# Values of the later chunks fetched by casting transfers of GpSimd in an attention and feed-forward kernel

## The chip, the cores and the metric

The kernel runs on one core of one Trainium2 chip. Time is device time of one execution, in microseconds (us). The engines have the names of the profile: PE (TensorE, matmuls) with PEld (its weight loads), DVE (VectorE), ACT (ScalarE), POOL (GpSimd) and SP (SyncE, which here only issues transfers). A transfer that SP or ACT issues is shown by the profile in a queue of kind hardware_dynamic (q1 for SP), one that POOL issues in q0, software_dynamic; both queues run on the same 16 DMA engines.

## The reference

Attention with two kinds of heads, then a gated feed-forward layer. Four batches, 8 heads, 768 positions, 64 values per head; heads 0, 2 and 6 see all earlier positions, the others ("streaming") see only the first 4 positions (the sink) and the last 64 (the window).

```python
scores = scale * np.matmul(q, k.transpose(0, 1, 3, 2))
stream_keep = causal & (is_sink | in_win)
mask = np.where(retr[0, :, 0, 0, None, None], full_mask, stream_mask)
scores = np.where(mask[None, :, :, :], scores, -1000000000.0)
a = np.exp(scores - max)
a = a / (np.sum(a, axis=-1, keepdims=True) + 1e-09)
attn_out = np.matmul(a, v)
x = attn_out.transpose(0, 2, 1, 3).reshape(B * S, H * D)   # 3072 x 512
h = x @ w_in                                               # 512 x 2048
g = h * (1.0 / (1.0 + np.exp(-beta * h)))
out = g @ w_out                                            # 2048 x 512
```

Inputs and output are float32; the products run in bfloat16.

## The kernel before

The 3072 rows are cut into 8 chunks of 384 positions: half a sequence of one batch each, in the order (batch 0, first half), (1, first), (0, second), (1, second), then the same for batches 2 and 3. Chunks are numbered from 0, so the fourth is chunk 3. Each chunk has 4 units, a unit being a pair of heads: unit u belongs to chunk u // 4. For each unit there is a step QK (scores, `steps_QK`, matmuls of line 451), an exponential on ACT into `es` (lines 458 and 460), masks by products on DVE (lines 478 to 496), a step PV (`steps_PV`, matmuls of line 532 into `po`), and a division by the sums (lines 541 and 545) into `x`. `x` is transposed into `xT` by a transfer of SP (line 560). Then the feed-forward layer of the chunk: `steps_G1` (line 600, gate in lines 605 and 608) and `steps_G2` (line 653), and an output by SP (line 659).

The order on the engines is written out. Up to unit 7 the string `RAMP` names each step by a word; from unit 8 on a loop runs over t = 8 to 33 and the string `PLAN` has a row for each t: the QK of unit t and the PV of unit t - 1 ("V", "p") are mixed with feed-forward steps of earlier chunks ("a", "b"). Work of the other engines is put off with `later(delay, fn)`: it is emitted once an estimated clock of the matmul stream has gone on by `delay` ns, or when the first step that needs it forces it. Each engine, and SP's and POOL's queue of transfers, then runs its own list in order; the semaphores between them are set by the framework. Eight transfers of one kind can be under way before the next waits for the oldest's semaphore.

What the change touches:

- Values. `VX[b % 2]` holds the values of a batch in bfloat16: six tiles of 128 positions, 8 heads, 64 values and a 65th column of ones, so the 64 values of one head stand 130 bytes from those of the next. `load_v` (line 132) has SP fetch a tile of 128 positions in float32 into the stage `vs` (256 KB); `cast_v` (line 251) casts it into `VX`, on an engine that the plan names, for chunk 3 on DVE and for chunks 4 to 7 on POOL (`values_at`).
- Sink blocks. `VO[b % 2]` holds for the streaming heads copies of value tiles in which the first 4 positions are replaced by the sequence's first 4. `sink_values` makes them on POOL: lines 259 (one copy of 128 partitions for each tile) and 260 (the 4 rows). A chunk of a first half has one block, of a second half three.
- Keys and queries of chunks 3 to 7. `load_rows` (line 282) has POOL fetch them by casting transfers, twelve a chunk, 64 KB as written, into buffers `ROWS[c % 2]` (named `s` in the profile, after the stage whose memory they use). `transposes_dma` (lines 294 and 297) has SP transpose them into `KT` and `QTD`. A row load into a buffer waits until the transposes that read it have run.
- Readers. PV of a unit reads `VX` and `VO` (line 532); the first unit of a chunk (heads 0 and 2) reads only `VX`, the second is the first to read `VO`.

In the loop before the change, chunk c's value tile i is loaded by SP at t = 4c - 4 + i (delay 2500) and cast at t = 4c - 3 + i (delay 3000); with the third cast come the sink copies. Chunk 3's loads stand in `RAMP` (words `lv3.0g lv3.1 lv3.2`).

Of the kernel before, what the change touches and what calls it, by code (L numbers as in the profile page):

```python
# [18 lines left out]
def kernel(  # L19
# [13 lines left out]
    nc = tc.nc  # L33
    B, H, S, D = q.shape
# [4 lines left out]
    HALF = S // 2  # L39
    HT = HALF // 128  # L40
    NPAIR = H // 2
    NU = B * 2 * NPAIR
    NCHUNK = B * 2

    retr = [1, 0, 1, 0, 0, 0, 1, 0]
    n_sink_i = 4
# [26 lines left out]
    def later(delay, fn):  # L73

        todo = [fn]

        def once():
            if todo:
                todo.pop()()
        heapq.heappush(heap, (clock[0] + delay, count[0], once))  # L80
        count[0] += 1
        return once
# [5 lines left out]
    def step(s):  # L88
        cost, fn = s
        flush(clock[0])  # L90
        clock[0] += cost
        fn()


    chunks = [(b0 + i, h2) for b0 in range(0, B, 2) for h2 in range(2) for i in range(2)]
# [27 lines left out]
    def load_v(c, held=False, tiles=range(HT)):  # L123
        b, h2 = chunks[c]
        if tiles[0] == 0:
            staged["v", c] = stage.tile([128, HT, H, D], F32, name="vs")
        vs = staged["v", c]
        if held:
            nc.gpsimd.memset(vs[:, :, 0, 0:1], 0.0)
        for t in tiles:  # L130
            r = h2 * HALF + t * 128
            nc.sync.dma_start(out=vs[:, t], in_=v[b, :, r:r + 128, :].rearrange("h p d -> p h d"))  # L132
# [68 lines left out]
    VX = [kvp.tile([128, 2 * HT, H, D + 1], BF16, name=f"VX{b}") for b in range(2)]  # L201
# [38 lines left out]
    def cast(u, name, copy):  # L240
        b, h2, p = units[u]
        c = u // NPAIR
        s = st_u.setdefault(u, {})
        if "qkb" not in s:
            s["qkb"] = att.tile([128, 2, HT, 2, D], BF16, name="qkb", bufs=4)
        copy(out=s["qkb"][:, "qk".index(name)], in_=staged[name, c, p // 2][:, p % 2:4:2].rearrange("p h t d -> p t h d"))

    def cast_v(c, t, copy):

        b, h2 = chunks[c]  # L250
        copy(out=VX[b % 2][:, h2 * HT + t, :, 0:D], in_=staged["v", c][:, t])  # L251

    def sink_values(c):
        b, h2 = chunks[c]
        ka, kz = (1, 2) if h2 == 0 else (2, 5)
        vx, vo = VX[b % 2], VO[b % 2]
        copy = nc.gpsimd.tensor_copy if c < 2 else nc.gpsimd.tensor_copy
        for i in range(ka, kz):
            copy(out=vo[:, i - 1, :, 0:D], in_=vx[:, i, :, 0:D])  # L259
        copy(out=vo[0:n_sink_i, ka - 1:kz - 1, :, 0:D],  # L260
             in_=vx[0:n_sink_i, 0:1, :, 0:D].to_broadcast([n_sink_i, kz - ka, H, D]))

    chunk_values = {2: []}

    def values_at(c, t, delay):
        def go():
            cast_v(c, t, nc.vector.tensor_copy if c < 4 else nc.gpsimd.tensor_copy)
            if t == HT - 1:
                sink_values(c)
        chunk_values.setdefault(c, []).append(later(delay, go))  # L270

    def sinks_at(u, delay):
        st_u[u]["sinks"] = later(delay, lambda: sinks_of(u))
# [43 lines left out]
    def transpose_qk(u, name):  # L317

        s = st_u.setdefault(u, {})
        tp = ps_m.tile([128, 512], F32, name="mm").bitcast(BF16)[:, 0:HALF].rearrange("p (t j) -> p t j", t=HT)  # L320
        for t in range(HT):
            nc.tensor.transpose(tp[:, t, :], s["qkb"][:, "qk".index(name), t].rearrange("p h d -> p (h d)"), ident)  # L322
        s["t" + name] = tp
# [351 lines left out]
    h = FO // 2  # L675
# [10 lines left out]
    def run(steps):  # L686
        for x in steps:
            step(x)

    copies = {"v": nc.vector.tensor_copy, "a": nc.scalar.copy, "g": nc.gpsimd.tensor_copy}  # L690
# [5 lines left out]

    def do(word):

        what, n, i, eng = re.fullmatch(r"([a-z]{2}|[a-z][A-Z])(\d*)\.?(\d*)([vag]?)", word).groups()
        n, i = int(n or 0), int(i or 0)  # L700
        if what in ("ck", "cq"):
            cast(n, what[1], copies[eng])
        elif what in ("tk", "tq"):
            step((170, lambda: transpose_qk(n, what[1])))
        elif what in ("kk", "kq"):
            copy_qk(n, what[1], copies[eng])
        elif what == "ko":
            sinks_of(n)
        elif what in ("ad", "qk", "ex", "ma"):
            if n not in visits:  # L710
                visits[n] = steps_QK(n)
            step((0 if what in ("ex", "ma") else 170, lambda: visits[n][what](i)))
        elif what == "cv":
            cast_v(n, i, copies[eng])
        elif what == "vo":
            sink_values(n)
        elif what == "pv":
            pv = products.setdefault(n, [])
            if not pv:
                pv.extend(steps_PV(n))  # L720
            run(pv[:2])
            del pv[:2]
        elif what == "no":
            normalize(n)
        elif what == "xd":
            x_by_dma(n)
        elif what == "xx":
            run(steps_X(n))
        elif what == "cx":
            copy_x(n, copies[eng])  # L730
        elif what == "on":
            ones_v(engines[eng], n)
        elif what == "ne":
            negatives([(0, 1, 2), (3, 4)][n])
        elif what == "be":
            step((100, beta_go))
        elif what == "lv":
            load_v(n, held=eng == "g", tiles=[i])
        elif what == "lq":
            load_qk(n, i, held=eng == "g")  # L740
        elif what == "wi":
            load_w_in(n)
        elif what == "wo":
            load_w_out(n)
        elif what == "rq":
            rows_queries()
        elif what == "rk":
            rows_keys()
        elif what == "ro":
            if n not in more_rows:  # L750
                more_rows[n] = load_rows(n)
            more_rows[n].pop(0)()
        elif what in ("dk", "dq"):
            transposes_dma(n, what[1])
        elif what == "ml":
            late[n].pop(0)()
        elif what == "tt":
            run(steps_T(n))
        elif what == "zz":
            keep_busy(n)  # L760
        elif what == "hm":
            opened.append(done[0])
            done[0] += 1
            step(halves[0](opened[-1], 0))
        elif what == "hf":
            step(halves[0](opened.pop(0), 1))
        else:
            feed({"mm": "a", "mA": "A", "mb": "b"}[what])

    def feed(x):  # L770
# [19 lines left out]
        qk3.1 no1 pv2 ck6v ex3.0 cq5v ck5g pv2 tk6 xx0 ad4.0 cq6g pv3 kq4v ex3.1 pv2 ad4.1 cx0v ad5.0 qk4.1 pv3 lv2.2  # L790
        no2 on1g tq5 pv3 qk4.0 kk6a ml0 tk5 cq7g kq5v ex4.1 kk5a ko5 ko6 ad5.1 tq6 wi1 qk5.0 ex4.0 tk7 tq7 ex5.0 no3
        qk5.1 ex5.1 kq6v xx1 ad6.0 kk7v wi2 kq7v wi3 cx1a qk6.0 ml1 ad6.1 ex6.0 cv1.1g ko7 qk6.1 cv1.0v ex6.1 hm lq2.1
        ma5.0 ma5.1 mm cv1.2g vo1 mm wo0 pv4 lv3.0g ad7.0 lv3.1 pv4 hf pv4 no4 qk7.0 ad7.1 pv5 pv5 ex7.0 lv3.2 qk7.1
        pv5 no5 ml1 wo1 ex7.1 pv6 pv6 wo2 mm pv7 rq pv7 pv7 no7 wo3 pv6 no6 rk cq8g xx2 ro3 cx2a mA mA ck8g xx3 cx3a
        mm mA mm mA mm mm mA mm mm mm mA mm ro3 mm mm mA mm mm mm ro3 mA mm ro3 mA mm ro3 mm mm ro3 mA mA mb mb tt8 mb
        mb mb
# [36 lines left out]
    for t in range(8, NU + 2):  # L833
        c, i = (t + 5) // NPAIR, (t + 5) % NPAIR
        if t >= 14 and c < NCHUNK and i < 3:
            for x, f in enumerate(load_rows(c)[4 * i:4 * i + 4]):
                later(1000 + 1500 * x, f)
        c, i = (t + 4) // NPAIR, (t + 4) % NPAIR
        if t >= 12 and c < NCHUNK and i < HT:
            later(2500, lambda c=c, i=i: load_v(c, tiles=[i]))  # L840
        c, i = (t + 3) // NPAIR, (t + 3) % NPAIR
        if t >= 9 and c < NCHUNK and i < HT:
            values_at(c, i, 3000)
        if t > 14 and t % NPAIR == 2 and t // NPAIR + 1 < NCHUNK:
            transposes_dma(t // NPAIR + 1)
        if 12 <= t + 1 < NU:
            sinks_at(t + 1, 1000)
        qk = steps_QK(t) if t < NU else []
        pv = steps_PV(t - 1) if 8 <= t - 1 < NU else []
        xx = steps_X(5) if t == 13 else steps_X(NU // 2 - 1) if t == NU + 1 else []  # L850
        tr = steps_T(t + 1) if t + 1 < 12 else []

        plan = PLAN[t - 8]
        for x in plan.split():
            if x == "V":
                run(qk[:1])
                qk = qk[1:]
            elif x == "p":
                run(pv[:1])
                pv = pv[1:]  # L860
            elif x == "T":
                run(tr)
                tr = []
            elif x == "X":
                run(xx)
                xx = []
            elif len(x) > 1:
                do(x)
            else:
                feed(x)  # L870
        run(qk + tr + xx + pv)
    i = 0
# [39 lines left out]
```

## Time and profile before

| what | us |
|---|---|
| median of 3 runs (lowest, highest) | 228.2 (228.14, 228.51) |
| the profiled execution | 228.94 |
| its span, first to last instruction | 227.0 |
| PE busy in the span | 219.4 |
| ACT busy | 154.0 |
| DVE busy | 142.1 |
| POOL busy | 87.3 |

The granted clock of PE was 0.999 over the span. In the groups of the profile a row has the line, engine and operation, what is written and read, how often, the busy time and mean ns of one, and after the second bar the idle time of the engine just before these instructions with what ended it. In the DMA view a queue's row has its packets, megabytes and the time of its packets as a share of the 16 engines' time; packets overlap, so shares can add up to over 100%. In a timeline a row has the start, the length, and in brackets the idle time before. In the view of waits the numbers are the total, how often, and the longest.

### The profile page before, as it was taken

How to read it: one execution, taken by the hardware profiler on the slowest of the kernel's cores; microseconds unless marked ns; L12 is line 12 of the kernel's file. 1: busy time of each engine (PE TensorE's matmuls, PEld its weight loads, DVE VectorE, ACT ScalarE, POOL GpSimd, SP SyncE). 2: the span in 40 equal slices, each digit the busy share in tenths (PEclk: the TensorE clock that was granted, in tenths of full speed). 3: DMA queues.
4: the chain of work that ended last, by engine and by line, in shares of the span. 5: the costliest groups of instructions: out<-in, count | busy, mean ns of one | idle time of the engine just before them, and what ended most of it. 6: DMA issues, size and time to landing. Idle time of an engine off the chain costs nothing.

```text
span 227.0 us, 5019 instructions
## 1 busy us (share of the span) xinstructions
PE 219.4 (97%) x1898; PEld 126.4 (56%) x1917; DVE 142.1 (63%) x342; ACT 154.0 (68%) x254; POOL 87.3 (38%) x143
## 2 busy tenths in 40 slices
PE   7989999999999999999999999999999999999994
PEld 3555766654655665556654664556645655456553
DVE  4679888852684779357932699646963779028600
ACT  2698898946767897449933887569876878139621
POOL 5377952249163399143064049910670000000000
PEclk9999999999999999999999999999999999999999
DMA  6999999999999899989869779596963030111012
GB/s 204 262 301 239 225 197 198 195 220 171 149 216 178 161 153 144 141 175 133 103 131 162 126 151 140 92 133 103 216 64 107 24 81 0 49 46 46 0 49 92
DMA packets 95383, 31.66 MB, mean 139 GB/s; under 512 B 81776, under 2 KB 92416, under 8 KB 95360
## 3 DMA queue, kind: packets, MB, share of 16 engines
q1 hardware_dynamic: 58880, 22.82, 50.2%
q0 software_dynamic: 35904, 8.13, 41.9%
q10 hardware_dynamic: 576, 0.40, 0.6%
q8 instruction: 15, 0.25, 0.5%
q14 instruction: 8, 0.07, 0.1%
HBM read 27.27 MB, written 6.29 MB: 148 GB/s over the span
## 4 chain that ended last, share of the span: by engine, by line
PE 89%; DMA 4%; DVE 2%; SPq 2%; issue 1%; ACT 0%; ACTq 0%; DVEq 0%
PE mm L653 34%; PE mm L600 25%; PE sp L600 12%; PE sp L451 6%; PE po L532 6%; DMA s<-in_k_dram 3%; DMA s<-in_q_dram 2%; PE mm L638 2%; DVE es L478 1%; PE mm L322 1%; SPq L132 1%; PE mm L570 1%; PE mm L451 1%; SPq L119 1%; PE sp L422 1%
## 5 line engine op out<-in xcount | busy, mean ns | idle before, releaser
L653 PE MATMUL mm<-w_out_sb,gT 128*128 128x512 bf16 x349 | 84.1, 379 | 1.3 <-issue 0.5
L460 ACT ACTIVATE es<-sp 128x768 bf16<-128x768 f32 (+2 forms) x72 | 56.5, 837 | 19.6 <-PE sp L451 19.4
L600 PE MATMUL mm<-xT,w_in_sb 128*128 128x384 bf16 x348 | 64.6, 326 | 0.0
L600 PEld LDWEIGHTS <-w_in_sb 128*128 128x128 bf16 x512 | 47.8, 98 | 29.7 <-issue 0.2
L605 ACT ACTIVATE th<-mm,beta_h 128x384 f32<-128x384 f32 x87 | 49.8, 588 | 5.6 <-PE mm L600 0.9
L653 PEld LDWEIGHTS <-gT 128*128 128x128 bf16 x368 | 33.4, 98 | 36.0 <-issue 1.5
L608 DVE SCALAR_TENSOR_TENSOR gT<-th,mm 128x384 bf16<-128x384 f32 x87 | 46.8, 551 | 7.4 <-ACT th L605 3.8
L282 POOL DMA_DIRECT2D s<-in_q_dram x30 | 22.4, 761 | 27.2 <-DMA QTD<-s 21.7
L600 PE MATMUL sp<-xT,w_in_sb 128*128 128x384 bf16 x164 | 32.3, 326 | 0.0
L657 ACT ACTIVATE osb<-mm 128x512 f32<-128x512 f32 x23 | 13.8, 602 | 26.1 <-PE mm L653 25.8
L532 PEld LDWEIGHTS <-es 128*128 128x128 bf16 x472 | 23.3, 98 | 13.6 <-issue 1.5
L608 DVE SCALAR_TENSOR_TENSOR gT<-th,sp 128x384 bf16<-128x384 f32 x41 | 22.3, 552 | 5.6 <-ACT th L605 3.7
L532 PE MATMUL po<-VX,es 128*128 128x65 bf16 x360 | 24.9, 194 | 0.8 <-ACT VX L251 0.4
L605 ACT ACTIVATE th<-sp,beta_h 128x384 f32<-128x384 f32 x41 | 23.8, 586 | 2.3 <-PE sp L600 0.2
L282 POOL DMA_DIRECT2D s<-in_k_dram x30 | 22.4, 759 | 6.8 <-DMA w_out_sb<-in_moe_w_out_dram 5.2
L251 POOL CAST VX<-vs 128x512 bf16<-128x512 f32 x16 | 10.6, 662 | 34.6 <-DMA vs<-in_v_dram 31.8
L541 DVE RECIPROCAL rec<-po 128x6 f32<-128x6 f32 x28 | 5.4, 193 | 27.0 <-PE po L532 27.0
L478 DVE TENSOR_TENSOR es<-es,Mh 128x768 bf16<-128x768 bf16 (+1 forms) x26 | 17.4, 698 | 5.0 <-ACT es L460 4.4
L451 PE MATMUL sp<-QTD,KT 64*128 64x128 bf16 (+2 forms) x258 | 19.2, 240 | 0.6 <-ACT QTD L333 0.3
L545 DVE TENSOR_TENSOR x<-po,rec 128x384 bf16<-128x384 f32 x28 | 15.6, 557 | 1.0
L451 PEld LDWEIGHTS <-KT 64*128 64x128 bf16 x278 | 11.1, 94 | 5.8 <-issue 3.6
L259 POOL COPY VO<-VX 128x512 bf16<-128x512 bf16 x16 | 10.0, 649 | 7.3 <-DVE VX L251 7.3
(74 smaller groups left out, 157.2 us busy)
## 6 DMA issues: line engine op xcount, KB each, us to landing
vs<-in_v_dram SPq DMA_DIRECT2D x24, 256.0 KB, 5.5
out_dram<-osb SPq DMA_DIRECT2D x23, 256.0 KB, 2.8
w_in_sb<-in_moe_w_in_dram POOLq DMA_DIRECT2D x4, 512.0 KB, 9.7
w_out_sb<-in_moe_w_out_dram POOLq DMA_DIRECT2D x4, 512.0 KB, 16.5
s<-in_k_dram POOLq DMA_DIRECT2D x30, 64.0 KB, 4.8
s<-in_q_dram POOLq DMA_DIRECT2D x30, 64.0 KB, 5.1
s<-in_k_dram SPq DMA_DIRECT2D x4, 384.0 KB, 6.8
s<-in_q_dram SPq DMA_DIRECT2D x4, 384.0 KB, 8.6
```

The lines of the kernel that those rows point to most:

```text
L251: copy(out=VX[b % 2][:, h2 * HT + t, :, 0:D], in_=staged["v", c][:, t])
L282: nc.gpsimd.dma_start(out=ROWS[c % 2, name][:, t, i * 4 * D:(i + 1) * 4 * D].rearrange("p (h d) -> p h d", d=D), in_=src[b, i:H:2, r:r + 1 ...
L451: nc.tensor.matmul(sps[i][r][:, x * 128:y * 128], key(a, lhs), s["QT"][half(a), qi * 128:(qi + y - x) * 128], start=first, stop=first or y ...
L460: nc.scalar.activation(out=views[i].rearrange("p r k j -> p r (k j)"), in_=banks[2][:, :, 0:n * 128], func=ACTF.Exp, scale=scale)
L478: nc.vector.tensor_mul(ev[:, :, 0:n], ev[:, :, 0:n], Mh[h2][:, None, m0:m0 + n].to_broadcast([128, 2, n, 128]))
L532: nc.tensor.matmul(po[:, qi, hh, :], e, val, start=(j == 0), stop=(j == len(lst) - 1))
L545: nc.vector.tensor_mul(xg[g][:, :, :, u % 2, :].rearrange("p a t d -> p t a d"), po[:, :, :, 0:D], rec.to_broadcast([128, HT, 2, D]))
L600: nc.tensor.matmul(hp[:, 0:HALF], w_in_sb[:, mo, fi * 128:(fi + 1) * 128], xT[c][:, mo, :], start=(mo == 0), stop=(mo == MO - 1))
L605: nc.scalar.activation(out=th, in_=hp[:, 0:HALF], func=ACTF.Tanh, scale=beta_h[:, fi:fi + 1])
L608: nc.vector.scalar_tensor_tensor(out=gTs[c][:, fi, :], in0=th, scalar=1.0, in1=hp[:, 0:HALF], op0=ALU.add, op1=ALU.mult)
L653: nc.tensor.matmul(op, gTs[c][:, fi, ns * 128:(ns + 1) * 128], w_out_sb[:, fi, :], start=(fi == 0), stop=(fi == FO - 1))
L657: nc.scalar.activation(out=osb, in_=op, func=ACTF.Copy, scale=0.5)
```

## The change

Chunks 3 to 7 no longer use `load_v` and `cast_v`. `fetch_v` has POOL fetch a value tile from the float32 input straight into `VX` by one casting transfer. `sink_values` for these chunks makes no copies: for each block POOL issues one transfer of partitions 4 to 127 and one of the 4 sink rows, both from the input. `values_at` issues the value transfers where the casts stood, and the sink blocks are issued by `sink_values_at` at t = 4c. The words `lv3` fall from `RAMP`, the value loads from the loop. Chunks 0 to 2 stay as they were.

```diff
+    def fetch_v(c, t):
+
+        b, h2 = chunks[c]
+        r = h2 * HALF + t * 128
+        nc.gpsimd.dma_start(out=VX[b % 2][:, h2 * HT + t, :, 0:D], in_=v[b, :, r:r + 128, :].rearrange("h p d -> p h d"))
+
     def sink_values(c):
         b, h2 = chunks[c]
         ka, kz = (1, 2) if h2 == 0 else (2, 5)
         vx, vo = VX[b % 2], VO[b % 2]
-        copy = nc.gpsimd.tensor_copy if c < 2 else nc.gpsimd.tensor_copy
+        if c > 2:
+            for i in range(ka, kz):
+                for lo, hi, r in ((n_sink_i, 128, i * 128), (0, n_sink_i, 0)):
+                    nc.gpsimd.dma_start(out=vo[lo:hi, i - 1, :, 0:D], in_=v[b, :, r + lo:r + hi, :].rearrange("h p d -> p h d"))
+            return
+        copy = nc.gpsimd.tensor_copy
         for i in range(ka, kz):
             copy(out=vo[:, i - 1, :, 0:D], in_=vx[:, i, :, 0:D])
...
     def values_at(c, t, delay):
-        def go():
-            cast_v(c, t, nc.vector.tensor_copy if c < 4 else nc.gpsimd.tensor_copy)
-            if t == HT - 1:
-                sink_values(c)
-        chunk_values.setdefault(c, []).append(later(delay, go))
+        chunk_values.setdefault(c, []).append(later(delay, lambda: fetch_v(c, t)))
+
+    def sink_values_at(c, delay):
+        chunk_values.setdefault(c, []).append(later(delay, lambda: sink_values(c)))
...
-        ma5.0 ma5.1 mm cv1.2g vo1 mm wo0 pv4 lv3.0g ad7.0 lv3.1 pv4 hf pv4 no4 qk7.0 ad7.1 pv5 pv5 ex7.0 lv3.2 qk7.1
+        ma5.0 ma5.1 mm cv1.2g vo1 mm wo0 pv4  ad7.0  pv4 hf pv4 no4 qk7.0 ad7.1 pv5 pv5 ex7.0  qk7.1
...
-        c, i = (t + 4) // NPAIR, (t + 4) % NPAIR
-        if t >= 12 and c < NCHUNK and i < HT:
-            later(2500, lambda c=c, i=i: load_v(c, tiles=[i]))
         c, i = (t + 3) // NPAIR, (t + 3) % NPAIR
         if t >= 9 and c < NCHUNK and i < HT:
             values_at(c, i, 3000)
+        if 12 <= t < NU and t % NPAIR == 0:
+            sink_values_at(t // NPAIR, 2500)
```

After the change the lines from 254 on stand some ten lower: the transfers are in lines 257 and 266, the row loads in 292, the matmuls of PV in 542.

More of the change, by code (lines that the diff above doesn't have):

```diff
@@ L697, in do @@
     def do(word):
-        what, n, i, eng = re.fullmatch(r"([a-z]{2}|[a-z][A-Z])(\d*)\.?(\d*)([vag]?)", word).groups()
+        what, n, i, eng = re.fullmatch(r"([a-z]{2}|[a-z][A-Z])(\d*)\.?(\d*)([vagd]?)", word).groups()
         n, i = int(n or 0), int(i or 0)
@@ L713, in do @@
         elif what == "cv":
-            cast_v(n, i, copies[eng])
+            fetch_v(n, i) if eng == "d" else cast_v(n, i, copies[eng])
         elif what == "vo":
```

## The prediction

> **What bounds the kernel now.** I read the page first: busy shares, slices, queues, chain, groups.
>
> ```profile
> span 227.0 us, 5019 instructions
> PE 219.4 (97%) x1898; PEld 126.4 (56%) x1917; DVE 142.1 (63%) x342; ACT 154.0 (68%) x254; POOL 87.3 (38%) x143
> PE   7989999999999999999999999999999999999994
> DMA  6999999999999899989869779596963030111012
> q0 software_dynamic: 35904, 8.13, 41.9%
> PE 89%; DMA 4%; DVE 2%; SPq 2%; issue 1%; ACT 0%; ACTq 0%; DVEq 0%
> L251 POOL CAST VX<-vs 128x512 bf16<-128x512 f32 x16 | 10.6, 662 | 34.6 <-DMA vs<-in_v_dram 31.8
> ```
>
> TensorE is busy for 219.4 of 227.0 us and makes 89% of the chain; the slices put most of its idle 7.6 us into the start and the end, which the change leaves alone. So a change of POOL's and SP's work can win only what TensorE waits for in between, and can lose whatever it makes TensorE wait for. POOL stands 31.8 us for value loads, but POOL is at 38%: that costs nothing by itself. The DMA slices are at 9 for most of the first half, so the queues have little to give.
>
> Next the view of waits, and around TensorE's one late wait the timelines and VectorE's line:
>
> ```profile
> PEld L532 <- DVE es L478: 0.9, 1, 0.9
> PEld L451 <- DVE VX L251: 0.4, 1, 0.4
> 139.51 4.15 DVE L478 TENSOR_TENSOR es<-es,Mh 128x768 bf16<-128x768 bf16 x2
> 139.90 1.75 POOL L259 COPY VO<-VX 128x512 bf16<-128x512 bf16 x3
> 141.71 1.68 POOL L260 COPY VO<-VX 4x1536 bf16<-4x1536 bf16 x1
> 142.12 0.24 PE L532 MATMUL po<-VX,es 128*128 128x65 bf16 x2 [0.36 <-DVE es L478]
> L478 DVE TENSOR_TENSOR es<-es,Mh x26: 418/554/2553, 21.6 to 187.6; 128x768 bf16<-128x768 bf16 x21, 128x512 bf16<-128x512 bf16 x5
> ```
>
> Two mask products of VectorE take 4.15 us where the median of one is 0.554, just while POOL copies the sink blocks of chunk 6, and TensorE stands 0.36 us. The weight loader's 0.9 and 0.4 us lie mostly beside running matmuls.
>
> **The change part by part.** Matmuls and ScalarE's work keep their order.
>
> *Removed:* fifteen value loads from SP's queue, twelve casts and the sink copies of chunks 3 to 7 from POOL, three casts from VectorE. What TensorE gets back is the 0.36 us above. The rest lay beside its work: I put it at 0, bounded by 0.4 us for the one weight load that waited for a VectorE cast. POOL's stalls on value loads go too, and some row loads start earlier; nothing on TensorE waited for those. SP issues transposes and outputs that much sooner, also 0.
>
> *Added, on POOL's queue:* fifteen value transfers (128x8x64) and twenty-two for sink blocks (eleven of 124 partitions, eleven of 4). Price per unit: a row load of 128x4x64 is 512 packets plus 16 for completion (60 of them and eight weight loads of as many, 68 x 528, make 35904, the number in q0's row). The DMA view of 85 to 95 us, where row loads stood in line, the source view of row loads, and the DMA view of 142 to 155 us, where the other queue was full too:
>
> ```profile
> q0 software_dynamic: 5581, 0.69, 109.8%
> L282 POOL DMA_DIRECT2D s<-in_q_dram x30: 742/750/800, 44.5 to 161.4; - x30
> DMA to landing us min/median/max: 2.9/3.6/4.9
> DMA  0100000019999756999999999989999999999992
> q0 software_dynamic: 3714, 0.46, 60.9%
> q1 hardware_dynamic: 3616, 1.11, 55.7%
> ```
>
> 5581 packets in 10 us are 558 per us: one row load drains in 528/558 = 0.946 us; call that a unit. A value transfer is 1024+16 packets and a sink block in two parts 1024+32, two units each. POOL's part is 0.75 us per 512 packets, at most 1.5 for a value transfer: issue is faster than draining and isn't the limit. In all the queue gets 52 units more, 49 us beside the 57 it has for rows. From 44.5 to 161.4 us, the first and last query row, it has 117 us for them: it fits on average, so only bursts count.
>
> *Where a burst meets TensorE.* Chunks 3 to 5 have wide cover. For chunk 3:
>
> ```profile
> 55.46 0.78 POOL L282 DMA_DIRECT2D s<-in_k_dram  x1
> 75.00 0.71 PE L532 MATMUL po<-VX,es 128*128 128x65 bf16 x18
> ```
>
> The three value transfers follow the row load of 55.46; taking four units in line before them, they land by about 55.46 + 2.9 + 10 x 0.946 = 68, and are read at 75.0. Chunk 6 is the tight one, because POOL must first wait for the transposes of chunk 6's queries, in both kernels:
>
> ```profile
> 132.84 1.48 POOL L282 DMA_DIRECT2D s<-in_q_dram  x2 [10.97 <-DMA QTD<-s]
> 134.31 0.63 POOL L251 CAST VX<-vs 128x512 bf16<-128x512 f32 x1
> 146.49 0.71 PE L532 MATMUL po<-VX,es 128*128 128x65 bf16 x18
> 147.57 0.54 PE L532 MATMUL po<-VX,es 128*128 128x65 bf16 x12
> 154.59 0.19 PE L532 MATMUL po<-VO,es 128*128 128x65 bf16 x1
> 155.36 0.19 PE L532 MATMUL po<-VO,es 128*128 128x65 bf16 x1
> 156.79 0.19 PE L532 MATMUL po<-VO,es 128*128 128x65 bf16 x1
> ```
>
> From 132.84 on POOL issues, in the changed program's order: two query rows, two value transfers, two query rows, two key rows, the third value transfer, four key rows, three sink blocks, three query rows. The first row lands at 132.84 + 2.9 = 135.7. The third value block is 11 units later: 146.1; it is read from 147.57, or 147.2 with the 0.36 us won. The key rows end at 149.9; the sink blocks land at 151.8, 153.7 and 155.6, and are read at 154.59, 155.36 and 156.79, less 0.36. All fit, the last by 0.8 us. Query rows of chunk 7 land by about 158.5 and are transposed until some 164; after the second transpose POOL issues the rest. The last value block of chunk 7 lands near 173, its sink blocks at 175 to 179:
>
> ```profile
> 175.29 0.95 PE L532 MATMUL po<-VX,es 128*128 128x65 bf16 x26
> 178.63 0.19 PE L532 MATMUL po<-VO,es 128*128 128x65 bf16 x1
> 180.12 0.19 PE L532 MATMUL po<-VO,es 128*128 128x65 bf16 x1
> ```
>
> These fit by 1.5 to 3 us. The unknown is the unit. A new piece lands 130 bytes from the next, where the row pieces are contiguous, and no row shows such a write. Below: 0.946 us, or less, since 1024 of the value packets of q1 no longer compete between 142 and 155 us. Above: between 142 and 155 us q0 moved 3714 packets in the 30 of 40 slices in which DMA was busy, 9.75 us: 381 per us, 1.39 us a unit. I take 0.95 to 1.0, nearer the first, because q1 is lighter than in either stretch.
>
> *The sum.* Profiled execution: 227.0 - 0.36 + 0 = 226.6 us of span. It took 228.94 in all (1.9 outside the span), so 228.6 for such an execution; the median of the runs, 228.2, is 0.7 below it, and by it the sum is 227.8. I say 227.9, for TensorE's separate waits on fifteen value transfers and twenty-two sink parts instead of one counter. Within 0.2% (0.46 us) is what a measurement can't tell from no change.
>
> **The rivals.**
>
> *The casting queue decides (slower).* Place: the third value block and the last sink block of chunk 6. From 135.7 there are 21 units to 156.4, so above 0.986 us a unit TensorE waits; only 4% above my value. At 1.1 us: 135.7 + 23.1 - 156.4 = 2.4 us. At 1.39 the value block lands at 151.0 (3.8 us late) and the last sink block at 164.9 (4.7 us more), with a few more in chunks 3 and 4: about 236 to 238. For it: the thin margin and the unaligned writes. Against: fewer packets on q1. Middle: 230.
>
> *Blocks of 124 partitions run on few of the 16 engines (slower).* 124 divides by 4, not by 8 or 16. On four engines a block is 248 packets each at 16/558 = 28.7 ns, 7.1 us instead of 1.8. Chunk 6: first block at 149.9 + 7.1 = 157.0 (2.8 us late), the third, if on the same four, at 164.1 (4.9 more); chunk 7 pays about 6 again, chunk 4's queries some 3 behind chunk 3's blocks: 228 + 8 to 17, say 240. No row shows a transfer whose partitions 16 doesn't divide, for or against.
>
> The Trainium skill ("DMA: Bandwidth & Descriptors", section "Why a DMA increments its semaphore by 16 and not by 1") has this rule: the number of engines is the largest up to 16 that divides the slowest dimension of both sides, which would make it four here. It also notes an exception for some plain copies from GpSimd, which get all 16. By the rule the sum would be 240, by the exception 227.9; no run here shows either yet.
>
> *More comes back (faster).* Should the weight loader's 0.9 and 0.4 us be real stalls, the gain is 1.3 us: 226.9. Against: the matmul's own row shows 0.36 us of idle, no more.
>
> *It doesn't do what it says:* POOL's wait of 10.97 us is for transposes, not values, and stays; that is in the sum already.
>
> **How the numbers follow.** Fits: 0.36, 227.9 (its own range 227.4 to 228.6). Queue decides: 0.30, 228.5 to 236. Few engines: 0.24, 236 to 245. More comes back: 0.10. Faster by over 0.2%: 0.10 and a seventh of the first, 0.15. Same: three quarters of the first and a tenth of the second, 0.30. Slower: the rest, 0.55. The range 227.4 to 238 leaves out a little below and most of the third case, under 2 in 10.
>
> **What would show it.** Right: L478's longest falls from 2.553 to about 0.6; the wait of 0.36 us before the matmul at 142.1 is gone; value transfers land 1.9 us apart; no wait of TensorE for DMA. Wrong: waits of L542 for transfers of `in_v_dram` near 147, 155 and 180 us (the queue), landings of sink blocks 7 us or more after their neighbours (few engines), or a unit over 1 us in the DMA view of 133 to 157 us.

## The result, and the profile after

The changed kernel takes 249.5 us (median of 6 runs, 246.72 to 251.85); the kernel before, on the same chip, 228.3 (6 runs, 228.12 to 229.12). The ratio is 1.086, with a 95% interval of 1.081 to 1.090: slower, and outside the predicted range. The medians, here and below, are of all executions and 21.2 us apart, while the ratios and their intervals leave out executions over 1.5% above the fastest of their kernel, and by the ratio the loss is 19.6 us. The profiled execution below is the longest of the six (251.85 us).

From the page of the changed kernel: span, busy shares, slices, the casting queue and the chain.

```profile
span 250.1 us, 5036 instructions
PE 229.8 (92%) x1917; PEld 129.1 (52%) x1917; DVE 141.3 (56%) x339; ACT 154.7 (62%) x254; POOL 109.9 (44%) x151
PE   7999999999895999989999999746999499999994
PEclk9999999999999799999999999985899769999999
DMA  7999999999999999999936899999999802021012
q0 software_dynamic: 96912, 11.68, 89.7%
PE 63%; DMA 24%; POOL 6%; DVE 3%; ACT 2%; issue 1%; SPq 0%; DVEq 0%; ACTq 0%
```

TensorE's idle time is no longer only at the two ends: the slices show holes near 80, 165 and 195 us, and behind each the granted clock falls. DMA, 4% of the chain before, is 24%. The queue has 96912 packets where the prediction's own prices give some 63000 (35904 and 52 units of 528).

What TensorE waits for in the changed kernel (line, cause, us in total, times, longest):

```profile
PE mm L610 <- DMA xT<-x: 7.7, 3, 3.6
PE po L542 <- DMA VO<-in_v_dram: 5.3, 2, 3.3
...
PE sp L610 <- DMA xT<-x: 0.8, 1, 0.8
```

The larger part, 7.7 and 0.8 us, is not a wait for anything that the change touches. `xT` is the transposed input of the feed-forward layer, and SP issues those transposes into the other queue, q1. The views of the two sources, first the sink blocks' transfers and then the transposes:

```profile
L266 POOL DMA_DIRECT2D VO<-in_v_dram x22: 586/1364/2172, 61.4 to 187.8; - x22
DMA to landing us min/median/max: 7.2/10.4/15.5
...
L570 SPq DMA_TRANSPOSE xT<-x x10: 1218/1630/3961, 69.1 to 207.0; - x10
...
DMA to landing us min/median/max: 2.7/6.2/11.7
```

and the same transposes in the kernel before:

```profile
L560 SPq DMA_TRANSPOSE xT<-x x10: 1211/1220/2192, 67.9 to 183.8; - x10
...
DMA to landing us min/median/max: 2.7/5.1/7.2
```

A transfer for a sink block lands 10.4 us after its issue in the median, 15.5 at worst; the prediction had put the blocks of chunk 6 two units, 1.9 us, behind one another. The slowest transpose went from 7.2 to 11.7 us. GpSimd itself stood still for these landings, 6.4 us before row loads and 2.8 us before a value transfer (POOL in the view of waits), so its later issues slipped too. The chain shows each of them carrying the end (start, us, what):

```profile
69.14 11.71 DMA xT<-x
...
157.11 13.76 DMA VO<-in_v_dram
...
188.33 10.73 DMA xT<-x
```

TensorE's timeline through chunk 6, the tight place of the prediction (start, us, form and count, in brackets the idle time before):

```profile
161.61 1.14 PE L610 MATMUL mm<-xT,w_in_sb 128*128 128x384 bf16 x6 [1.34 <-DMA xT<-x]
...
165.57 0.20 PE L542 MATMUL po<-VO,es 128*128 128x65 bf16 x1 [2.05 <-DMA VO<-in_v_dram]
...
170.92 0.24 PE L542 MATMUL po<-VO,es 128*128 128x65 bf16 x1 [3.29 <-DMA VO<-in_v_dram]
...
171.03 2.75 PE L610 MATMUL mm<-xT,w_in_sb 128*128 128x384 bf16 x8
...
179.12 1.46 PE L610 MATMUL mm<-xT,w_in_sb 128*128 128x384 bf16 x8
```

The value blocks are not waited for; the sink blocks are. And the stalls cost twice: the eight matmuls at 171.03 take 2.75 us, the same eight at 179.12 take 1.46. The windows view of the three stretches in which the granted clock was at half (busy time of PE, PEld, DVE, ACT and POOL, then the granted clock, DMA share, GB/s):

```profile
81.22:84.64 3.42, 3.42 (x12) 1.63 (x11) 1.23 (x4) 1.17 (x3) 2.36 (x4) 0.50 1.94 204
166.56:176.80 10.24, 6.95 (x26) 3.13 (x25) 2.50 (x6) 3.27 (x6) 1.16 (x2) 0.50 1.55 81
197.28:204.10 6.82, 5.00 (x23) 2.61 (x23) 1.66 (x3) 1.74 (x3) 0.00 (x0) 0.50 0.17 37
```

TensorE is busy for 15.4 us in them, at half rate, which is 7.7 us more than the same work takes at a full clock. The first began behind a stall of 2.69 us that ended at 80.89, the second at 166.56, behind the stall of 2.05 us and before the one of 3.29, and the third during the stall of 3.63 us that ended at 199.10. The Trainium skill ("TensorE: Matmul & The Clock Gate", section "Part 1: The HAM clock gate (the "warmup" mystery)") says that the array's clock is halved after an idle window of about 3.4 us and comes back after a busy window as long. The half rate agrees (1.46 / 2.75 = 0.53). The idle time does not: here the clock fell behind stalls of 2.69 and 2.05 us. It stayed down for 3.4, 10.2 and 6.8 us; in the second stretch TensorE had been at work without a gap from 170.92 on, 5.9 us, when the clock came back.

### The profile page after: what moved, and what is told of

It reads as the page before. It is cut to its first block, busy times and chain, and to the rows that moved or that the text cites. A ratio compares the mean times of both kernels' runs of the same rounds, so it can differ in the third digit from the quotient of the medians.

```text
span 250.1 us, 5036 instructions
## 1 busy us (share of the span) xinstructions
PE 229.8 (92%) x1917; PEld 129.1 (52%) x1917; DVE 141.3 (56%) x339; ACT 154.7 (62%) x254; POOL 109.9 (44%) x151
## 3 DMA queue, kind: packets, MB, share of 16 engines
q0 software_dynamic: 96912, 11.68, 89.7%
## 4 chain that ended last, share of the span: by engine, by line
PE 63%; DMA 24%; POOL 6%; DVE 3%; ACT 2%; issue 1%; SPq 0%; DVEq 0%; ACTq 0%
PE mm L663 21%; PE mm L610 19%; DMA xT<-x 13%; PE sp L610 10%; DMA VO<-in_v_dram 6%; PE sp L461 4%; PE po L542 3%; DMA KT<-s 3%; POOL VO L266 2%; DMA s<-in_k_dram 2%; POOL s L292 2%; PE mm L648 1%; PE mm L332 1%; PE sp L432 1%; DVE gT L618 1%
## 5 line engine op out<-in xcount | busy, mean ns | idle before, releaser
L663 PE MATMUL mm<-w_out_sb,gT 128*128 128x512 bf16 x368 | 86.0, 380 | 0.0
L610 PE MATMUL mm<-xT,w_in_sb 128*128 128x384 bf16 x348 | 69.6, 342 | 7.7 <-DMA xT<-x 7.7
L610 PEld LDWEIGHTS <-w_in_sb 128*128 128x128 bf16 x512 | 49.9, 102 | 42.6 <-issue 15.2
L610 PE MATMUL sp<-xT,w_in_sb 128*128 128x384 bf16 x164 | 35.2, 346 | 0.9 <-DMA xT<-x 0.8
L542 PEld LDWEIGHTS <-es 128*128 128x128 bf16 x472 | 23.7, 99 | 20.8 <-DMA VO<-in_v_dram 6.4
L266 POOL DMA_DIRECT2D VO<-in_v_dram x22 | 29.0, 1346 | 0.7 <-DMA s<-in_q_dram 0.4
L542 PE MATMUL po<-VX,es 128*128 128x65 bf16 x360 | 25.1, 195 | 0.4 <-ACT VX L251 0.4
L551 DVE RECIPROCAL rec<-po 128x6 f32<-128x6 f32 x28 | 6.5, 231 | 29.1 <-PE po L542 29.1
L488 DVE TENSOR_TENSOR es<-es,Mh 128x768 bf16<-128x768 bf16 (+1 forms) x26 | 13.7, 557 | 5.6 <-ACT es L470 5.0
L542 PE MATMUL po<-VO,es 128*128 128x65 bf16 x72 | 11.2, 200 | 6.0 <-DMA VO<-in_v_dram 5.3
L257 POOL DMA_DIRECT2D VX<-in_v_dram x15 | 13.5, 912 | 5.1 <-DMA VO<-in_v_dram 2.8
```

What stands on the lines that cost most here:

```text
L266: nc.gpsimd.dma_start(out=vo[lo:hi, i - 1, :, 0:D], in_=v[b, :, r + lo:r + hi, :].rearrange("h p d -> p h d"))
L488: nc.vector.tensor_mul(ev[:, :, 0:n], ev[:, :, 0:n], Mh[h2][:, None, m0:m0 + n].to_broadcast([128, 2, n, 128]))
L542: nc.tensor.matmul(po[:, qi, hh, :], e, val, start=(j == 0), stop=(j == len(lst) - 1))
L610: nc.tensor.matmul(hp[:, 0:HALF], w_in_sb[:, mo, fi * 128:(fi + 1) * 128], xT[c][:, mo, :], start=(mo == 0), stop=(mo == MO - 1))
L663: nc.tensor.matmul(op, gTs[c][:, fi, ns * 128:(ns + 1) * 128], w_out_sb[:, fi, :], start=(fi == 0), stop=(fi == FO - 1))
```

## The experiments

Before the runs, two theories. A: the transfers of 124 partitions run on 4 of the 16 DMA engines (the prediction's second rival). B: the amount of work in the casting queue, with pieces 130 bytes apart (its first rival). All medians are of 4 or 10 runs, beside runs of the kernel before on the same chip (228.4 to 228.7); ratios are to these, with 95% intervals.

How the queue's pieces are counted below: data makes 4096 pieces for the weights, 60 x 512 for rows, 15 x 1024 for values and 11 x 1024 for sink blocks, 61440 in all, and each transfer adds 16 of 4 bytes for its completion. What a page's q0 row has beyond these needs another explanation. In the changed kernel that is 96912 - 61440 - 105 x 16 = 33792 pieces of 4 bytes, or 3072 for each of the eleven blocks.

**The same bytes, cut at a multiple of 16.**

```diff
-                for lo, hi, r in ((n_sink_i, 128, i * 128), (0, n_sink_i, 0)):
+                for lo, hi, r in ((16, 128, i * 128), (n_sink_i, 16, i * 128), (0, n_sink_i, 0)):
```

> The same bytes go by the same queue; only the transfer of 124 partitions is cut into one of 112 and one of 12 (the 4 sink rows stay a transfer of their own). Theory A (few engines: a transfer of 124 partitions runs on 4 of the 16 DMA engines): the large part lands in line with its neighbours, within 7 us of its issue where it took 8.4 to 15.5, TensorE no longer waits for VO or for xT transposes, the 4-byte packets of q0 fall from 35472 to under 5000, and the time is 227.5 to 230. Rival B (the amount: 52 units more in the queue, in pieces 130 bytes apart): the data packets stay 57344 of 128 bytes, so 247 to 252.

Measured: 228.6 us, ratio 1.001 (0.998 to 1.004). Its page, its windows, and its sink transfers:

```profile
span 229.0 us, 5056 instructions
PE 221.0 (96%) x1917; PEld 126.4 (55%) x1917; DVE 136.7 (60%) x339; ACT 154.1 (67%) x254; POOL 103.6 (45%) x162
...
q0 software_dynamic: 64704, 11.55, 68.3%
```

```profile
53.00:139.00 86.00, 85.86 (x772) 48.76 (x771) 51.38 (x141) 60.46 (x100) 50.09 (x67) 1.00 1.45 139
139.00:157.00 18.00, 18.00 (x168) 9.62 (x167) 9.52 (x29) 12.87 (x20) 15.09 (x21) 1.00 1.85 138
157.00:177.00 20.00, 20.00 (x177) 11.23 (x174) 12.67 (x31) 15.20 (x25) 10.87 (x15) 1.00 1.20 130
```

```profile
L266 POOL DMA_DIRECT2D VO<-in_v_dram x33: 578/695/952, 63.3 to 173.5; - x33
...
DMA to landing us min/median/max: 3.4/5.2/7.7
```

All 21 us are gone with one line. TensorE is busy for 123.86 of the 124 us between 53 and 177 at a full clock, with every value and sink block still coming by the casting queue. B falls: the data pieces are the same 57344 of 128 bytes. The longest landing, 7.7 us, is a little above the 7 expected of it. Of 4-byte pieces 64704 - 61440 = 3264 are left.

The two pages also divide the loss. Both have 1917 matmuls: TensorE is busy 229.8 - 221.0 = 8.8 us longer in the changed kernel (7.7 of it in the three stretches at half clock), and idle for 250.1 - 229.8 = 20.3 us against 229.0 - 221.0 = 8.0, so 12.3 us of stalls. Together 21.1, the difference of the spans. Both profiled executions are the longest of their kernel.

**One half of the change at a time.** First the values alone, with the sink blocks copied by POOL as before (`sink_values` without its new branch):

> Values by casting transfers as in the changed kernel; the sink blocks are copied by GpSimd from the value blocks as before. A (few engines): 227.5 to 229, the 15 value transfers of 128 partitions land about 1 us apart where they stand in line. B (amount): 30 of the 52 added units remain, 30/52 of 21.2 us, so 240.

Measured: 229.4 us, ratio 1.004 (1.002 to 1.006). Then the sink blocks alone, with values loaded by SP and cast as before (the new branch of `sink_values` put into the kernel before, called where the change calls it):

> Values loaded and cast as before; only the sink blocks come by transfers of 124 and 4 partitions. A (few engines): nearly the whole loss, 243 to 250, with waits of TensorE for VO and for xT. B (amount): 22 of the 52 units remain, 22/52 of 21.2 us, so 237.

Measured: 252.6 us, ratio 1.104 (1.095 to 1.113). The queue's row of the values alone, then queue and waits of the sink blocks alone:

```profile
q0 software_dynamic: 51504, 10.10, 57.6%
```

```profile
q0 software_dynamic: 81312, 9.71, 66.0%
...
PE mm L606 <- DMA xT<-x: 6.5, 3, 2.7
PE po L538 <- DMA VO<-in_v_dram: 3.4, 1, 3.4
PE sp L457 <- DMA QTD<-s: 3.2, 2, 1.9
```

The sink blocks alone cost all of it and 3 us more, a little over A's upper end. With 15 SP loads back in q1, TensorE now also waits for the transposes of queries (QTD); that the loads are why was not tried. Values by transfer carry no extra piece: 4096 + 30720 + 15360 of data and 16 for each of 68 + 15 = 83 transfers make 51504, the row's number exactly. The sink blocks alone make 4096 + 30720 + 11264 and 90 x 16, which leaves 33792 of 81312, as in the changed kernel. Values with POOL's copies are 0.8 us above the time before and 0.4 above A's upper end. The profiled execution shows a wait of 1.1 us for an xT transpose there; whether that is all of the 0.8 was not tried. The value transfers of chunk 3 land 1.1 and 1.4 us apart there, near the 1 us expected.

**What rule sets the number of engines.** Two other cuts of the same rows. 120 divides by 15 and not by 16:

```diff
+                for lo, hi, r in ((n_sink_i, 124, i * 128), (124, 128, i * 128), (0, n_sink_i, 0)):
```

> Each sink block cut into 120, 4 and 4 partitions (120 divides by 15, not by 16). Divisor rule (a transfer runs on the largest number of engines up to 16 that divides its partitions, and each engine without a share gets one 4-byte piece for each of a sharing engine's pieces, as 11 x (32 + 96) + 1856 = 3264 fits the cut into 112, 12 and 4): 120 on 15 engines, so 11 x (64 + 96 + 96) + 1856 = 4672 four-byte pieces in q0, and the time of the cut into 112 and 12, 228 to 229.5. Rival (only powers of two, 120 on 8 engines): 11 x (960 + 192) + 1856 = 14528 pieces, blocks land 3 us later, 229 to 233.

and 62 divides by 2 and by 31:

```diff
+                for lo, hi, r in ((n_sink_i, 66, i * 128), (66, 128, i * 128), (0, n_sink_i, 0)):
```

> Each sink block cut into 62, 62 and 4 partitions. Divisor rule: 62 on 2 engines, 248 pieces on each as with 124 on 4, so cutting a transfer doesn't help: landings 8 us and more after issue, 11 x (2 x 14 x 248 + 96) + 1856 = 79296 four-byte pieces, time 246 to 256. Rival (the length of one transfer matters, not its partitions): 62 rows land in half the time, 230 to 238.

Measured: 120, 4 and 4 take 229.0 us, ratio 1.000 (0.997 to 1.003); 62, 62 and 4 take 275.4, ratio 1.206 (1.196 to 1.216). The queue's row of the first:

```profile
q0 software_dynamic: 66112, 11.55, 71.7%
```

and of the second its queue, its waits and its sink transfers:

```profile
q0 software_dynamic: 140736, 11.85, 91.2%
...
PE po L542 <- DMA VO<-in_v_dram: 15.2, 5, 7.2
PE mm L610 <- DMA xT<-x: 8.5, 3, 4.4
```

```profile
L266 POOL DMA_DIRECT2D VO<-in_v_dram x33: 592/2025/2171, 61.2 to 214.7; - x33
...
DMA to landing us min/median/max: 9.2/13.9/18.6
```

Less 61440, the rows leave 4672 and 79296 pieces of 4 bytes: the divisor rule's numbers to the piece, and not those of a rule of powers of two (14528). The trace's records of q0 have just as many pieces of 4 bytes. They do not name a piece's engine; how many engines there were is read from the counts. By these 120 partitions ran on 15 engines, 124 on 4 and 62 on 2, and every engine without a share got one 4-byte piece for each piece of a sharing engine: 12 x 248 + 12 x 8 = 3072 for a block of 124 and 4. Where a transfer begins is not the cause either: the 120 partitions begin at partition 4, as the 124 did. The time was above what was expected for 62: halving a transfer left 248 pieces on each of its engines and made twice as many transfers, and the loss went from 21 to 46.7 us. The counts bear out the Trainium skill's rule ("DMA: Bandwidth & Descriptors", section "Why a DMA increments its semaphore by 16 and not by 1"), the largest number up to 16 that divides the slowest dimension of both sides; its exception, all 16 for some plain copies of GpSimd, did not hold for these casting transfers. The two kernels also clear the small transfers of 4 partitions: on 4 engines too, and twice as many with the cut of 120, but with 8 pieces on each engine they cost nothing that shows.

**Where the loss arises.** The cut into 112 and 12, but with 124 partitions kept in some chunks:

```diff
+                cuts = ((n_sink_i, 128, i * 128),) if c == 6 else ((16, 128, i * 128), (n_sink_i, 16, i * 128))
+                for lo, hi, r in cuts + ((0, n_sink_i, 0),):
```

> As the cut into 112 and 12, except in chunk 6, whose three blocks keep 124 partitions. A with the loss where TensorE waits: chunk 6 alone had 1.3 + 2.1 + 3.3 us of waits between 160 and 171 us and some 3.5 us at a lower clock behind them, so about 10 us over the kernel with all blocks cut: 236 to 241. Rival (each block of 124 costs alike, 3 of 11): 3/11 of 21.2 us, so 234. B (amount): 247 to 252.

> 124 partitions only for the single sink blocks of chunks 4 and 5, else 112 and 12. If the loss lies where TensorE meets a late transfer: chunk 4 showed no wait there, chunk 5 0.8 us for an xT transpose, so 228.5 to 230.5. Rival (each block of 124 costs alike): 2/11 of 21 us, so 232.4.

> 124 partitions only for the three sink blocks of chunk 3, else 112 and 12. The changed kernel had lost 2.7 us of waiting for an xT transpose by 80.9 us and about as much again at a lower granted clock behind it: 232 to 235. If only waits for the sink blocks themselves cost (chunk 3 showed none): 228.5 to 229.5.

> 124 partitions only for the three sink blocks of chunk 7, else 112 and 12. If the losses of the chunks simply add: chunk 3 alone cost 5.4 us over before, chunks 4 and 5 together 4.4, chunk 6 8.1, so of the 21.2 us of the changed kernel 3.3 are left for chunk 7: 232. If chunk 7 alone costs what the changed kernel lost in it (3.6 us of wait for an xT transpose before 199.1, and about 3 us at a lower granted clock behind it): 235. In both the wait is again at the feed-forward block's xT, not at VO.

| 124 partitions in | blocks | us | before | ratio (95%) | loss by medians, us | loss by ratio, us |
|---|---|---|---|---|---|---|
| chunk 6 | 3 | 236.7 | 228.6 | 1.033 (1.026 to 1.039) | 8.1 | 7.5 |
| chunks 4 and 5 | 2 | 233.1 | 228.7 | 1.019 (1.011 to 1.027) | 4.4 | 4.3 |
| chunk 3 | 3 | 234.1 | 228.7 | 1.016 (1.003 to 1.028) | 5.4 | 3.6 |
| chunk 7 | 3 | 234.0 | 228.4 | 1.021 (1.016 to 1.026) | 5.6 | 4.7 |
| all (the changed kernel) | 11 | 249.5 | 228.3 | 1.086 (1.081 to 1.090) | 21.2 | 19.6 |

TensorE's late wait in each, by the waits views of chunk 6 alone, chunk 3 alone and chunk 7 alone:

```profile
PE po L543 <- DMA VO<-in_v_dram: 5.3, 2, 3.7
```

```profile
PE mm L611 <- DMA xT<-x: 2.6, 1, 2.6
```

```profile
PE mm L611 <- DMA xT<-x: 3.8, 1, 3.8
```

The parts add to 23.5 us by medians and 20.1 by ratios, near the whole either way. Chunk 3 is the least sure: two of its four executions, 231.0 and 233.8 us, make the ratio. Chunks 3, 6 and 7 went as the changed kernel's waits had said, chunk 6 at the low end and chunk 7 between its two figures. Chunks 4 and 5 did not: 228.5 to 230.5 was expected, because the changed kernel shows hardly a wait for a transfer there. The rival, 2.1 us for each block, was nearer. The timeline and the chain of that kernel say why:

```profile
115.67 0.81 PE L611 MATMUL sp<-xT,w_in_sb 128*128 128x384 bf16 x4 [3.21 <-DVE gT L619]
```

```profile
104.76 9.62 DMA KT<-s
...
114.50 0.20 DVE KO L323
114.70 0.94 DVE gT L619 x2
```

The wait is put down to VectorE. But VectorE was itself held: its KO copy needs the transposed keys, that transpose was issued at 104.76, behind the sink block of 102.05, and landed 9.62 us later; the gate of the feed-forward block (gT) stood behind the copy on VectorE. So a late transfer reached TensorE by way of VectorE, and a list of TensorE's waits for DMA leaves that out.

## Why the prediction was wrong, step by step

- *The step that failed* is "a sink block in two parts 1024+32, two units each". It counts pieces and takes them as spread over all 16 engines. A block of 124 partitions has its 992 pieces on four, by the counts above: 248 each. In the changed kernel the second and third block of chunk 3, issued at 64.06 and 66.67, land 10.96 and 15.32 us later, at 75.0 and 82.0, 7.0 us apart, which is 28 ns for each of 248 pieces (their view stands below this list). The second rival had priced 28.7 ns and 7.1 us. Not every gap is as long: neighbours land 1.9 and 7.0 us apart in chunk 3, 7.1 and 5.4 in chunk 6, 2.9 and 6.6 in chunk 7, and which four engines a block had is not known. What went wrong was the choice between the two: no row bore on it, and the exception was given as good a standing as the rule, with 0.24 for the rival and a range that ended below its time. The range also left out more than the "under 2 in 10" said of it: the faster case, 226.9 with 0.10, lies below it and most of the 0.24 above, together nearly 3 in 10.
- *The rival's size*, 240, was 9.5 us short. It priced the late sink blocks (7.7 us in chunk 6, where 2.05 + 3.29 = 5.3 was waited for them) and, at some 3 us, queries behind chunk 3's blocks. It had nothing for the other queue, whose transposes came late beside the sink blocks (8.5 us of waits for xT; that they stand behind the same engines is inferred), and nothing for the clock behind each stall (7.7 of 8.8 us more busy time).
- *"Chunks 3 to 5 have wide cover"* failed. The cover was reckoned to the reading of the values, which did arrive in time. What came late was work of q1: xT for chunk 3, keys for chunk 5. Those three chunks cost 8 to 10 us by themselves (the table).
- *The unit.* With the few engines gone, 0.946 us was too much, and the upper bound of 1.39 far too much. The rows are of the cut into 112 and 12, at the end of this section. The third value block, issued at 141.9, lands 5.0 us later, some 11 us after the first row's issue at 135.70, where 146.1 - 132.84 = 13.3 was predicted. From 139 to 157 us the queue moved 13055 pieces in 18 us, 725 per us, so 0.73 us for 528. Writes 130 bytes apart showed no price. The value transfers of chunk 3 land 0.7 and 0.9 us apart in the changed kernel, where the prediction's sign of being right was 1.9. The first rival (the queue decides, from 0.986 us a unit) is out.
- *The fits themselves hold once the cause is taken away.* No wait of TensorE for a transfer between 53 and 177 us, the tight chunk 6 included. The predicted 227.9 stands to the 228.2 before as 0.999, inside that kernel's interval.
- *Removed.* The longest mask product falls from 2.553 us to 0.826 in that kernel, and TensorE's wait of 0.36 us for it is gone. As a gain in time it can't be seen.
- *"Issue isn't the limit"* is right for values (mean 912 ns for 1024 pieces, where up to 1500 was allowed). A block of 124 took 2.1 us of POOL.
- *What would show it wrong* named the right signs: landings of sink blocks 7 us after their neighbours, and waits of L542 for `in_v_dram`. It lacked the waits for xT.

The sink transfers of the changed kernel issued from 64.06 to 66.67, two blocks and the 4 rows between them, whose landings are 11.0, 9.4 and 15.3 us after issue:

```profile
L266 POOL DMA_DIRECT2D VO<-in_v_dram x3: 591/2046/2068, 64.1 to 66.7; - x3
...
DMA to landing us min/median/max: 9.4/11.0/15.3
```

The rows of the cut into 112 and 12 for the steps above: POOL's timeline, the one value transfer issued at 141.9 in its source's view, the queue from 139 to 157 us (packets, megabytes, share), and the mask products:

```profile
135.70 1.48 POOL L292 DMA_DIRECT2D s<-in_q_dram  x2 [27.56 <-issue]
```

```profile
L257 POOL DMA_DIRECT2D VX<-in_v_dram x1: 952/952/952, 141.9 to 141.9; - x1
...
DMA to landing us min/median/max: 5.0/5.0/5.0
```

```profile
q0 software_dynamic: 13055, 1.58, 150.4%
```

```profile
L488 DVE TENSOR_TENSOR es<-es,Mh x26: 419/552/826, 23.4 to 189.7; 128x768 bf16<-128x768 bf16 x21, 128x512 bf16<-128x512 bf16 x5
```

## What to carry to other kernels

Before a casting transfer of GpSimd is given a number of partitions that 16 does not divide, find the largest number up to 16 that divides it: in these runs that many DMA engines carried its data, by the counts, and 124 as 112 and 12 took 21 us off with one line, where cutting it into two of 62 added 26. Transfers on few engines also made the other queue's transfers late (the slowest `xT` transpose landed after 11.7 us instead of 7.2), so look for their price in waits for transfers that the change doesn't touch. Transfers issued by SP or ACT, and plain copies, were not tried. The change without its transfers of 124 partitions is a draw (1.001, 0.998 to 1.004): no version here beats the kernel before, whose TensorE had only 0.36 us to win.

## What the runs showed of the hardware that was not expected

- Engines without a share of a transfer still get pieces of 4 bytes, one for each piece of a sharing engine: 33792 of them in the changed kernel, 77440 with 62 partitions. They swell the packet count, and by the trace's records they make 12.8 points of q0's 89.7% in the changed kernel and 29.4 of its 91.2% with 62. One takes 9 ns in the median, a piece of 128 bytes 32.
- The time that POOL needs to issue a transfer goes with the pieces of one engine, or with all pieces when those of 4 bytes are counted, and not with the bytes: 0.6 to 0.7 us at 8 pieces (4 partitions), 0.75 at 32 (a row), 0.9 to 1.1 at 64 (a value tile; 120 partitions), 2.1 at 248, and the same 2.0 for 62 partitions as for 124, with half the bytes.
- Stalls of 2 to 3 us were enough to halve TensorE's granted clock: it fell behind stalls of 2.69 and 2.05 us in the changed kernel and behind one of 2.59 us with 124 partitions in chunk 3 alone, and stayed at 0.50 for 3.4 us or more. Between the two profiled executions compared above 12.3 us of stalls came with 8.8 us more of busy time.
